# Another order of the operations of QKV, W1 and W2 on one Trainium2 core, and other staging rows in the last output block

## The chip, the cores and the metric

The kernel runs on one core of one Trainium2 chip. The time is the device time of one execution in microseconds (us). Before the change it was 1256.47 us, the median of three runs (1256.34 to 1257.6). A core has five engines with a queue of instructions each: TensorE (PE; its weight loads are shown apart as PEld), VectorE (DVE), ScalarE (ACT), GpSimd (POOL) and SyncE (SP). Each engine takes its queue strictly in order. An instruction waits for semaphores that other engines' instructions or DMA transfers raise. In this kernel SP issues nearly all transfers, and POOL issues those that add into DRAM.

## The reference

One batch of 2048 tokens with 576 channels, all in float32: a block of local attention and a block that mixes neighbouring tokens run beside each other on the same normalized input.

```python
def A(xn, wqkv, wo):      # 32 heads of 18; 8 keys back, 2 apart
    q, k, v = split(xn @ wqkv)                     # 576 -> 3 x 576
    kg, vg = k[s - 2*w], v[s - 2*w]                # w = 0..7
    attn = softmax(q . kg * 18**-0.5)              # masked where s - 2*w < 0
    return (attn . vg) @ wo                        # 576 -> 576

def B(xn, w1, w2, w3, w4):
    h = gelu(layernorm(xn) @ w1)                   # 576 -> 576
    hs = four channel quarters of h, shifted by +1, -1, +2, -2 tokens
    x1 = xn + hs @ w2
    return x1 + gelu(layernorm(x1) @ w3) @ w4      # 576 -> 4608 -> 576

xn = layernorm(x)
out = x + A(xn, wqkv, wo) + B(xn, w1, w2, w3, w4)
```

## The kernel before

**Arithmetic.** Operands of the matrix products are split into a high part (rounded to fp32r) and a low part (the rest), and a product of K rows is made from high x high, high x low and low x high. So each weight and each tile of x needs, ahead of its products: a load, a cast that gives the high part (ACT, L343 for weights, in the casts of x L579), and a subtraction that gives the low part (VectorE, L346 and L554 for weights, and for one main and one tail part at the start POOL by the same lines; VectorE, L581 and L585, for x). Rows 256 to 287 of each half of the 576 channels are the "tail" and are handled apart from the "main" rows (`wt`/`wu` for weights, `t`/`u` for x).

**Tiles.** The 2048 tokens are 16 tiles (rows of the buffer `Y`, [128, 16, 576]) of 128 tokens. For each tile of x: `x` loads it into its row of Y (SP, L298); `st` takes mean and variance (VectorE, L178 to L180) and the power -0.5 on POOL (L181); `no` normalizes in place (VectorE, L188); `ta` copies the tail channels into row 10 of Y (POOL, L362; `ta1a` on ACT); `tm` and `tt` turn main and tail through TensorE (L370, L374); `ch`, `cl`, `ct`, `cu` split the turned tile. The QKV products of tile t with a group of 432 columns are a "unit" `u`: 14 matmuls (L454), written as four parts `.0` to `.3`, then `o` (eviction from PSUM) and `s` (spill to DRAM by SP). `sc` works out the scales of the second layernorm for two tiles by seven small powers and products on POOL (L310 to L315). `sb` are four differences of weights on VectorE (L353), needed for the products of tile pairs (a Strassen-like scheme; `g6` to `g15`, TensorE L724), whose x operands are read back from DRAM (`gp`), and split again (`ph`, `pl`, `pt`, `pu`, `sx`). Then come W1 (`m`, `mg`, `mh`, `ml`), and W2 (`w0.0` and on). 39 transposes of an identity matrix (L478) run at the start ahead of the first product.

**What sets the order.** All of these operations are functions in a table `T`, and the string `ORDER_Q` (from L53) names 1108 of them in the order in which they are issued (`for name in ORDER_Q.split(): T[name]()`, L1098). That order is the order of each engine's queue. After QKV, W1 and W2 the attention and the main part of B (W3 and W4, the matmuls of L1306 and L1570, to about 1180 us) follow with an order of their own, which the change doesn't touch.

**The end.** W4's results for ten of the sixteen tiles are gathered in DRAM (`yd`): ACT evicts a partial sum from PSUM into a staging row of Y (L1311), and POOL issues a transfer that adds it to `yd` (L1312). In the last block of W3/W4 the staging rows are rows of Y that have no sum of their own at that time; `EV` holds them, and from the end of the first of its eight groups (`j == 0`) they are the rows in the tuple `rows`, taken round and round. Before that `EV` is (9, 11, 10, 2). `load_y` reads the gathered sums back into Y (SP, L1834). Then each tile of the output is the product with Wo (`mm_tok`, L272, 28 matmuls into one of three banks of PSUM), the addition of Y's row (VectorE, L1876) and the store (SP, L1877); the last tile is done in two halves (L1882).

Of the kernel before, what the change touches and what calls it, by code (L numbers as in the profile page):

```python
# [58 lines left out]
sb0.2 u4.0 u4.1 u4.2 u5.0 c1.2 wh1B11.0 tt4 tm5 ch5 u4.3 u4o u4s ct4 sb0.3 x9 cu4 u5.1 u5.2 tt5
u5.3 u5o u5s cl4 ct5 wl1B11.0 wh0T3.0 wl0T3.0 u6.0 u6.1 u6.2 u6.3 u6o u6s u7.0 aw2 wh0T1.0 u7.1  # L60
u7.2 u7.3 u7o u8.0 u9.0 u7s x6 u8.1 u8.2 x7 cu5 u9.1 wt0T3 wh0T3.1 u8.3 u8o u8s cl5 u9.2 u9.3
u10.0 wh1B11.1 st9 wl0T3.1 wu0T3 c3.0 u9o u10.1 c3.1 wt1B11 u10.2 u10.3 wl0T1.0 st6 u11.0 u10o u9s
u10s u11.1 u11.2 wh0T1.1 u11.3 u11o u11s wt0T1 c3.2 wh1B12.0 wl1B11.1 u12.0 u12.1 wu1B11 wh1B12.1
u12.2 u12.3 aw1 u12o u12s u13.0 u13.1 u13.2 u13.3 u13o x8 aw3 st7 sc6 no7 u14.0 u14.1 wl1B12.0
u13s u14.2 u15.0 u15.1 u14.3 no6 u15.2 u15.3 wl0T1.1 wu0T1 early zg6 zt6 zg7 zt7 zp3.1 u14o u14s
wl1B12.1 u16.0 wt1B12 zp3.3 wu1B12 zp3.2 sb1.0 st8 sb1.1 sb1.2 u16.1 u16.2 sb1.3 u16.3 u15o u16o
u17.0 u15s u17.1 u17.2 u17.3 no9 zp3.0 no8 aw4 u18.0 u18.1 wh1T1.0 u18.2 u18.3 wh1T3.0 wl1T3.0
u17o wl1T1.0 u16s u19.0 u19.1 u17s u18o u18s wt1T3 u19.2 sc8 zg8 u19.3 u19o u20.0 u20.1 u20.2
u20.3 u21.0 sc2 gp3.0 zt8 zg9 gp3.1 gp3.2 zt9 wh1T3.1 u21.1 gp3.3 gp3.4 u21.2 u20o u21.3 gp3.5
u21o ph3A11 wu1T3 ph3A22 zp4.2 u22.0 pl3A11 zp4.1 zp4.0 zp4.3 ph3A12 pl3A12 pl3A22 sx3.0 u19s  # L70
pt3A11 sx3.1 u23.0 pt3A22 u23.1 pt3A12 pu3A12 pu3A22 u22.1 u23.2 sx3.3 ph3S4 u23.3 u20s pl3S4
pt3S4 u22.2 pu3S4 u21s pu3A11 sx3.2 x10 u22.3 wt1T1 gp4.0 wu1T1 x11 gp4.1 gp4.2 gp4.3 gp4.4 gp4.5
ph3S1 pl3S1 pt3S1 pu3S1 wh1T1.1 wl1T1.1 aw0 u22o u23o u22s pt3S3 pu3S3 ph3S3 pl3S3 wl1T3.1 u23s
mid g6.1 g7.1 g6.5 g7.5 g6c g6.6 g6k5 g6.3 x12 g6k6 g7c g7k5 st10 st11 sc10 no10 zg10 g6.7 g6o7
g6s7 ph4A11 g6o3 g6s3 g6.2 g6o2 no11 g6s2 sx4.0 zt10 ph4A22 sx4.1 sx4.3 g7.6 g6.4 g7k6 g7.7 zg11
g6o4 pl4A11 zt11 g6s4 pt4A11 zg0 zp5.0 g7o7 zt0 zg1 pu4A11 sx4.2 g7.3 pt4A22 zp5.2 zt1 pt4S1 pu4S1
ph4S1 pl4S1 g7.2 g7o2 zg2 g7.4 g7o4 ph4A12 pl4A12 pu4A22 g7o3 pt4A12 pu4A12 g8.1 g9.1 g7s7 g8c
zp5.3 st12 zp5.1 x13 zt2 zp0.3 zp0.1 zp0.2 st13 zp0.0 sc12 gp5.0 pl4A22 gp5.1 gp5.2 sc4 gp5.3
gp5.4 gp5.5 g9c g8.5 g9.5 g9.6 g8.6 g7s2 g8.2 g8k5 pt4S3 pu4S3 ph4S3 pl4S3 x15 g8k6 g8.7 g9k5 g9k6
g8o2 g8s2 g7s4 x14 no13 no12 zg12 zt12 zg13 zt13 zp6.3 zp6.1 zp6.2 zp6.0 g8o7 zg3 g9.3 sx5.0 sx5.1  # L80
ph5S1 g8.3 g8o3 g8s3 ph5A12 g9.7 g9o7 sx5.2 ph5A11 g8.4 pl5A11 pl5S1 g9.2 g8o4 pt5A11 g7s3 g9s7
g8s7 sx5.3 pu5A11 pt5S1 g9.4 gp6.0 g9o2 st14 gp6.1 gp6.2 gp6.3 st15 g8s4 zt3 g9o4 pu5S1 g10.1
# [24 lines left out]
vh4 ml32 vl4 w0.0 rs2.3 w1.0 w1.1 mh33 mg33 ml33 w0.1 w2.0 w2.1 wy1 ws1 wy0 ws0 rs2.1 rs2.7 rg2.0
rg2.1 wy2 rg2.2 rg2.3 rp2.3 rs3.5 rs3.7 rp2.1 rs3.3 rs3.1 rg3.0 rp2.0 rg3.1 w3.0 w3.1 wy3 ws2
# [16 lines left out]
def fused_block(ctx, tc, x, wqkv, wo, w1, w2, w3, w4, out):  # L125
# [1789 lines left out]
```

## Time and profile before

| what | value |
|---|---|
| median of three runs | 1256.47 us (1256.34 to 1257.6) |
| the profiled execution, its own time | 1258.14 us |
| its span in the profile | 1256.3 us |
| TensorE busy | 99% of the span, 7361 matmuls |
| VectorE, ACT, POOL busy | 74%, 60%, 23% |
| transfers | 230.5 MB, 183 GB/s over the span |

The profile comes from one execution. A row of the timeline has the start in us, the length of the group in us, the engine, the line and operation, and the tiles that go out and in; in brackets stands how long the engine was idle before it and which engine and tile ended that. "x112" is 112 instructions in a row. A row of the stretches ("from:to") has the length, then busy time (and instructions) of PE, PEld, DVE, ACT and POOL in it, then the granted clock of TensorE (1.00 is the full clock), the share of the transfer engines, and GB/s. Lines such as L1834 are lines of the kernel before; in the changed kernel the string is a line shorter, so each line behind it has a number lower by one.

### The profile page before, as it was taken

To read this page: it belongs to the slowest core of one execution; us is meant where nothing else is said; L and a number is where in the kernel's file an instruction comes from. 1 tells how busy PE (TensorE), PEld (TensorE's weight loads), DVE (VectorE), ACT (ScalarE), POOL (GpSimd) and SP (SyncE) were. 2 spreads that over 40 slices of the span, in tenths; PEclk is the share of its full clock that TensorE was granted. 3 is DMA by queue.
4 is the path that set the end of the run, shared out by engine and by line. 5 is a ranking of instruction groups with operands and counts; after the bars stand their busy time and mean duration, and the time that the engine had idled before them with its cause. 6 is when DMAs were issued, how large, how long until landed. Compare 5 with 4: busy or idle time off the path is not lost.

```text
span 1256.3 us, 19980 instructions
## 1 busy us (share of the span) xinstructions
PE 1241.3 (99%) x7361; PEld 1144.4 (91%) x7361; DVE 931.6 (74%) x1182; ACT 759.4 (60%) x1234; POOL 285.7 (23%) x415
## 2 busy tenths in 40 slices
PE   8899999999999999999999999999999999999998
PEld 8899998899999999898899999989899999999998
DVE  7687554699458989997759898889999983554531
ACT  4456556437545545465868767776776776776610
POOL 4333100022231111111222232222232232222200
PEclk9999999999999999999999999999999999999999
DMA  7678897238788985859688998888867779899972
GB/s 211 175 183 204 191 226 213 53 113 254 183 220 195 214 168 123 168 125 255 124 180 187 211 190 191 196 167 210 235 132 178 135 140 195 175 221 229 259 226 86
DMA packets 221130, 230.50 MB, mean 183 GB/s; under 512 B 99544, under 2 KB 158136, under 8 KB 220904
## 3 DMA queue, kind: packets, MB, share of 16 engines
q1 hardware_dynamic: 188280, 162.43, 45.9%
q0 software_dynamic: 32752, 66.80, 32.7%
q8 instruction: 58, 0.95, 0.3%
q14 instruction: 40, 0.33, 0.1%
HBM read 130.76 MB, written 108.82 MB: 191 GB/s over the span
## 4 chain that ended last, share of the span: by engine, by line
PE 61%; issue 4%; DMA 4%; DVE 1%; ACT 1%; POOL 1%; SPq 0%; POOLq 0%; ACTq 0%; DVEq 0%
PE ps L1306 29%; PE cc L1570 18%; PE p L1270 10%; PE ps L272 3%; DMA yd<-Y 1%; DMA Y<-yd 1%; POOL yd L1312 1%; DMA w3st<-in_B_w_dram 1%; DMA w3s<-w3st 0%; DVE xt L970 0%; PE p L1882 0%; ACT Y L1250 0%; SPq L231 0%; DVE Y L1317 0%; DVE w3st L1403 0%
## 5 line engine op out<-in xcount | busy, mean ns | idle before, releaser
L1306 PEld LDWEIGHTS ps<-w,c 128*128 128x128 f32 x3456 | 477.8, 189 | 16.7 <-ACT Y L1311 1.6
L1306 PE MATMUL ps<-w,c 128*128 128x288 f32 x3456 | 487.3, 296 | 1.7 <-ACT Y L1311 0.9
L1312 POOL DMA_DIRECT2D yd<-Y x154 | 139.1, 906 | 366.9 <-ACT Y L1311 302.0
L1261 DVE TENSOR_TENSOR c<-Y,c 128x512 fp32r<-128x512 f32 x144 | 98.8, 687 | 87.9 <-ACT Y L1250 83.0
L1311 ACT COPY Y<-ps 128x576 f32<-128x576 f32 x154 | 97.9, 636 | 73.5 <-PE ps L1306 64.4
L1570 PE MATMUL cc<-xt,w3s 128*128 128x512 f32 (+1 forms) x504 | 127.2, 392 | 0.0
L1570 PEld LDWEIGHTS cc<-xt,w3s 128*128 128x128 f32 (+1 forms) x504 | 92.3, 188 | 17.3
L1314 ACT COPY Y<-ps 128x576 f32<-128x576 f32 x89 | 57.0, 641 | 59.0 <-PE ps L1306 57.2
L1181 DVE TENSOR_TENSOR po<-q,k 128x1152 f32<-128x1152 f32 (+1 forms) x48 | 84.2, 1755 | 0.8
L1570 PE MATMUL cc<-x1n,w3a 128*128 128x512 f32 (+1 forms) x336 | 84.7, 392 | 0.0
L1184 DVE TENSOR_REDUCE L<-po 128x64 f32<-128x1152 f32 (+1 forms) x48 | 84.0, 1751 | 0.8
L1249 ACT ACTIVATE c<-p 128x512 fp32r<-128x512 f32 x48 | 28.7, 598 | 89.1 <-PE p L1270 89.1
L1157 DVE TENSOR_TENSOR po<-v,L 128x1152 f32<-128x1152 f32 x56 | 75.4, 1354 | 0.9
L1580 DVE TENSOR_TENSOR Y<-cc,Y 128x512 f32<-128x512 f32 x49 | 33.7, 688 | 53.5 <-ACT Y L1576 47.5
L454 PE MATMUL p<-wb,xt 128*128 128x432 f32 (+1 forms) x336 | 70.9, 372 | 0.0
L1570 PEld LDWEIGHTS cc<-x1n,w3a 128*128 128x128 f32 (+1 forms) x336 | 60.4, 188 | 10.0
L454 PEld LDWEIGHTS p<-wb,xt 128*128 128x128 f32 (+1 forms) x336 | 65.5, 197 | 3.1
L1161 DVE TENSOR_TENSOR po<-po 128x1152 f32<-128x1152 f32 x49 | 66.4, 1355 | 0.9
L181 POOL TENSOR_TENSOR rs<-rs,mhalf 128x1 f32<-128x1 f32 x32 | 21.9, 686 | 170.1 <-DVE mv L184 97.0
L1287 ACT COPY ps<-Y 128x576 f32<-128x576 f32 x89 | 57.4, 645 | 3.1 <-DVE Y L1317 1.2
L724 PE MATMUL ca<-wb,xt 128*128 128x432 f32 (+1 forms) x280 | 58.9, 360 | 0.0
L724 PEld LDWEIGHTS ca<-wb,xt 128*128 128x128 f32 (+1 forms) x280 | 52.7, 189 | 2.6 <-ACT keep L731 0.2
(248 smaller groups left out, 2137.3 us busy)
## 6 DMA issues: line engine op xcount, KB each, us to landing
yd<-Y POOLq DMA_DIRECT2D x156, 288.0 KB, 6.1
Y<-in_B_w_dram SPq DMA_DIRECT2D x29, 576.0 KB, 5.7
w3st<-in_B_w_dram SPq DMA_DIRECT2D x56, 256.0 KB, 7.7
qkvd<-stg SPq DMA_DIRECT2D x44, 216.0 KB, 3.8
yd<-ev POOLq DMA_DIRECT2D x26, 288.0 KB, 6.5
w3st<-in_B_w_dram SPq DMA_DIRECT2D x92, 64.0 KB, 7.5
xd<-big SPq DMA_DIRECT2D x16, 320.0 KB, 5.6
Y<-in_A_x_dram SPq DMA_DIRECT2D x16, 288.0 KB, 3.8
```

What stands on the lines that cost most here:

```text
L454: pe.matmul(ps[:, :QB], xo[:n, o + k, a, :], W[:n, w + k, v, :], start=i == 0, stop=i == len(PLAIN) - 1)
L724: pe.matmul(ps, form(g // 2, x, n, a), W[:n, OP[w], v, :], start=start and i == 0, stop=stop and i == len(HALVES) - 1, skip_group_check=True)
L1157: dve.tensor_tensor(dst, vv, Lf[:, :, w:w + 1].to_broadcast([128, TPP * GH, HD]), op=ALU.mult)
L1161: dve.tensor_tensor(o, o, dst, op=ALU.add)
L1181: dve.tensor_tensor(dst, qf[:, None, :].to_broadcast([128, n, TPP * GC]), win, op=ALU.mult)
L1184: dve.tensor_reduce(Lw[:, w:w + n, :], dst.rearrange("p w (x d) -> p w x d", d=HD), axis=AX.X, op=ALU.add)
L1261: dve.tensor_tensor(h[:, 1, :], g, h[:, 0, :].bitcast(F32), op=ALU.subtract)
L1270: pe.matmul(ps, W3[f][:, w, :], x1n[b][:, a, :], start=n == 0, stop=n == len(PAIRS) - 1)
L1306: pe.matmul(ps[:, k, :HF], h[:, col], w[:, p, k * HF:(k + 1) * HF], start=n == 0 and not seed, stop=n == len(seq) - 1, skip_group_check=True)
L1311: act.copy(e.rearrange("p (h c) -> p h c", h=2), ps[:, :, :HF])
L1312: pool.dma_start(yd[t], e, accum_op=ALU.add)
L1570: pe.matmul(ps, WX[w][:k, v, SLOT[w], :], area[sb][xk][:k, a, :], start=onto is None and i == 0, stop=last and i == len(HALVES) - 1, skip_ ...
```

## The change

The string `ORDER_Q` is replaced as a whole. The same operations are named, in another order nearly everywhere. Its first lines are enough to see the kind:

```diff
 ORDER_Q = """
-x0 pw0 pw1 st0 x1 st1 no0 ta0 tm0 no1 tm1 x2 st2 c0.1 c0.0 zpad x3 c0.2 x4 c2.0 c2.1 c2.2 wh0B11.1
-wL0B11.1 ch0 no2 wh0B11.0 wl0B11.0 pw2 pw3 pw4 st3 tt0 cl0 ta2 tm2 ch1 cl1 x5 u0.0 ta1a u1.0 u1.1
...
+x0 st0 x1 st1 pw0 pw1 pw2 no0 x3 tm0 pw3 x2 pw4 c0.0 c0.1 c0.2 st2 ch0 x4 x5 c2.0 c2.1 c2.2
+wh0B11.0 ta0 tt0 st3 no1 tm1 wh0B11.1 no2 ct0 wl0B11.0 tm2 u0.0 ch1 u1.0 cl0 ta1a u0.2 cu0 no3 tm3
...
 """
...
         if j == 0:
             low_part(h21, Z4)
-            load_y((2, 5))
-            rows = (1, 3, 13, 15, 9)
+            load_y((1, 2, 5))
+            rows = (3, 13, 15, 9, 11)
             EV[0] = tuple(rows[(i - evc[0] - 1) % 5] for i in range(5))
...
         if j == 7:
-            load_y((1, 3))
+            load_y((3,))
```

The new order was made by a planner that takes VectorE and GpSimd to exclude each other; nothing in the kernel enforces that, and no wait is added for it. In the tail, row 1 is no longer a staging row from `j == 0` on; row 11 takes its place. Row 2 stands in `EV` ahead of `j == 0` as before. `load_y` of row 1 moves from the last group (`j == 7`) to the first.

Three places show what moves. In their rows Y_71 is the buffer Y, `wb0_125` the first weight buffer, `xt_...` the turned and split tiles of x, `ps_...` and `p1_...` are banks of PSUM, and the names in "waits" are the engines or transfer queues that are waited for.

**The start, on VectorE.** Before, rows 9 to 15 of its queue are the normalization of tiles 0 and 1, the statistics of tile 2, the normalization of tile 2, and the low part of the first weight's half:

```order
L188 TENSOR_SCALAR Y_71<-Y_71,mv0_78,rs0_81 128x576 [waits Pool_49] x2
L178 BN_STATS bn_84<-Y_71 128x6 [waits DMAHW2_49]
L178 BN_STATS bn_84<-Y_71 128x6
L179 BN_AGGR mv0_78<-bn_84 128x2 [waits DVE_49]
L180 TENSOR_SCALAR rs0_81<-mv0_78 128x1 [waits DVE_49]
L188 TENSOR_SCALAR Y_71<-Y_71,mv0_78,rs0_81 128x576 [waits Pool_49]
L346 TENSOR_TENSOR wb0_125<-rawa_221,wb0_125 128x864 [waits DMAHW4_49,Activation_49]
```

Now the statistics of tiles 3 and 2 stand between the normalization of tile 0 and that of tiles 1 and 2 (rows 9 to 19):

```order
L187 TENSOR_SCALAR Y_71<-Y_71,mv0_78,rs0_81 128x576 [waits Pool_49]
L177 BN_STATS bn_84<-Y_71 128x6 [waits DMAHW3_49]
L177 BN_STATS bn_84<-Y_71 128x6
L178 BN_AGGR mv0_78<-bn_84 128x2 [waits DVE_49]
L179 TENSOR_SCALAR rs0_81<-mv0_78 128x1 [waits DVE_49]
L177 BN_STATS bn_84<-Y_71 128x6 [waits DMAHW2_49]
L177 BN_STATS bn_84<-Y_71 128x6
L178 BN_AGGR mv0_78<-bn_84 128x2 [waits DVE_49]
L179 TENSOR_SCALAR rs0_81<-mv0_78 128x1 [waits DVE_49]
L187 TENSOR_SCALAR Y_71<-Y_71,mv0_78,rs0_81 128x576 [waits Pool_49] x2
L345 TENSOR_TENSOR wb0_125<-rawa_219,wb0_125 128x864 [waits DMAHW4_49,Activation_49]
```

So one more tile's statistics stand ahead of the normalization of tiles 1 and 2; the low part still follows the latter.

**Tiles 4 and 5, on POOL.** Before, the tail copies (L362) of tiles 4 and 5 stand apart, with the scale powers of tiles 0 and 1 (L310 to L315) between them (the first row is the power of tile 4):

```order
L181 TENSOR_TENSOR rs0_81<-rs0_81,mhalf_73 128x1 [waits DVE_49]
L362 COPY Y_71<-Y_71 128x256 [waits DVE_49,PE_49]
L181 TENSOR_TENSOR rs0_81<-rs0_81,mhalf_73 128x1 [waits DVE_49]
L310 TENSOR_TENSOR rs1_82<-rs0_81 128x2
L311 TENSOR_TENSOR rs1_82<-rs1_82,mv0_78 128x2 [waits Pool_49]
L312 TENSOR_TENSOR rs1_82<-rs1_82,eps_74 128x2 [waits Pool_49]
L314 TENSOR_TENSOR rs1_82<-rs1_82,mhalf_73 128x1 [waits Pool_49]
L315 TENSOR_TENSOR mv1_79<-rs1_82,half_75 128x1
L314 TENSOR_TENSOR rs1_82<-rs1_82,mhalf_73 128x1
L315 TENSOR_TENSOR mv1_79<-rs1_82,half_75 128x1
L362 COPY Y_71<-Y_71 128x256 [waits DVE_49,PE_49]
```

Now the power of tile 5 and both copies come first, and the power of tile 6 and the scale powers follow:

```order
L180 TENSOR_TENSOR rs0_81<-rs0_81,mhalf_73 128x1 [waits DVE_49]
L361 COPY Y_71<-Y_71 128x256 [waits PE_49,Pool_49]
L361 COPY Y_71<-Y_71 128x256 [waits DVE_49]
L180 TENSOR_TENSOR rs0_81<-rs0_81,mhalf_73 128x1 [waits DVE_49]
L309 TENSOR_TENSOR rs1_82<-rs0_81 128x2
L310 TENSOR_TENSOR rs1_82<-rs1_82,mv0_78 128x2 [waits Pool_49]
L311 TENSOR_TENSOR rs1_82<-rs1_82,eps_74 128x2 [waits Pool_49]
L313 TENSOR_TENSOR rs1_82<-rs1_82,mhalf_73 128x1 [waits Pool_49]
L314 TENSOR_TENSOR mv1_79<-rs1_82,half_75 128x1
L313 TENSOR_TENSOR rs1_82<-rs1_82,mhalf_73 128x1
L314 TENSOR_TENSOR mv1_79<-rs1_82,half_75 128x1
```

The copy of tile 5 has moved ahead of the seven small instructions. On PE, before, the tail turn of tile 4 (L374, ps_355), the main turn of tile 5 (L370, ps_437), eight products and the tail turn of tile 5 (ps_437) follow one another:

```order
L374 MATMUL ps_355<-ident_72,Y_71 128x128 [waits Activation_49,Pool_49]
L374 MATMUL ps_355<-ident_72,Y_71 128x128
L370 MATMUL ps_437<-ident_72,Y_71 128x128 [waits DVE_49,PE_49]
L370 MATMUL ps_437<-ident_72,Y_71 128x128 x3
L454 MATMUL p1_410<-wb0_125,xt_240 128x432 [waits DVE_49]
L454 MATMUL p1_410<-wb0_125,xt_240 128x432
L454 MATMUL p1_423<-wb0_125,xt_240 128x432 x6
L374 MATMUL ps_437<-ident_72,Y_71 128x128 [waits Activation_49,Pool_49]
L374 MATMUL ps_437<-ident_72,Y_71 128x128
```

Now the tail turn of tile 4 (L373, ps_339) and that of tile 5 (ps_378) have 28 products between them:

```order
L373 MATMUL ps_339<-ident_72,Y_71 128x128 [waits Pool_49]
L373 MATMUL ps_339<-ident_72,Y_71 128x128
L453 MATMUL p1_435<-wb0_125,xt_231 128x432 x8
L453 MATMUL p1_442<-wb0_125,xt_231 128x432 x6
L453 MATMUL p1_483<-wb0_125,xt_231 128x432 [waits Activation_49]
L453 MATMUL p1_483<-wb0_125,xt_231 128x432 x13
L373 MATMUL ps_378<-ident_72,Y_71 128x128 [waits Activation_49,Pool_49]
L373 MATMUL ps_378<-ident_72,Y_71 128x128
```

The tail turn of tile 5 has moved behind 20 more products; its main turn, now ps_378, stands further ahead and isn't among these rows.

**The tail, on SP.** Before, the reads of the gathered rows (L1834) stand in the order 2, 5, 7, 1, 3, with the reads of attention results (L231) between them:

```order
L231 DMA xt_11340<-xd_10773 128x3x512 [waits DMAHW2_49,PE_49]
L231 DMA xt_11340<-xd_10773 128x2x512 [waits DMAHW3_49]
L1834 DMA Y_71<-yd2_90 128x576 [waits DMASW5_49,DMAHW4_49,DMASW1_49,Activation_49]
L1834 DMA Y_71<-yd5_92 128x576 [waits DMAHW5_49,DVE_49]
L231 DMA x1n3_11530<-xd_11025 128x3x512 [waits DMAHW6_49,PE_49]
L231 DMA x1n3_11530<-xd_11025 128x2x512 [waits DMAHW7_49]
L1834 DMA Y_71<-yd7_93 128x576 [waits DMAHW0_49,DVE_49]
L231 DMA xt_11580<-xd_11244 128x3x512 [waits DMAHW1_49,PE_49]
L231 DMA xt_11580<-xd_11244 128x2x512 [waits DMAHW2_49]
L1834 DMA Y_71<-yd1_89 128x576 [waits DMAHW3_49,DMASW6_49,Activation_49]
L1834 DMA Y_71<-yd3_91 128x576 [waits DMAHW4_49,DMASW7_49,Activation_49]
```

Now row 1 is read ahead of row 2, and only row 3 stays at the end:

```order
L230 DMA xt_11340<-xd_10773 128x3x512 [waits DMAHW2_49,PE_49]
L230 DMA xt_11340<-xd_10773 128x2x512 [waits DMAHW3_49]
L1833 DMA Y_71<-yd1_89 128x576 [waits DMAHW4_49,DVE_49]
L1833 DMA Y_71<-yd2_90 128x576 [waits DMASW5_49,DMAHW5_49,DMASW1_49,Activation_49]
L1833 DMA Y_71<-yd5_92 128x576 [waits DMAHW6_49,DVE_49]
L230 DMA x1n3_11531<-xd_11025 128x3x512 [waits DMAHW7_49,PE_49]
L230 DMA x1n3_11531<-xd_11025 128x2x512 [waits DMAHW0_49]
L1833 DMA Y_71<-yd7_93 128x576 [waits DMAHW1_49,DVE_49]
L230 DMA xt_11581<-xd_11244 128x3x512 [waits DMAHW2_49,PE_49]
L230 DMA xt_11581<-xd_11244 128x2x512 [waits DMAHW3_49]
L1833 DMA Y_71<-yd3_91 128x576 [waits DMAHW4_49,DMASW6_49,Activation_49]
```

Row 1's read has moved past seven others, and it waits for VectorE and a transfer queue now, no longer for ACT's eviction into that row.

More of the change, by code (lines that the diff above doesn't have):

```diff
@@ L59 @@
[L59 to L82, printed above, removed]
```

97 lines of the change are left out of this document (60 added, 37 removed).

## The prediction

> **What bounds the kernel now.** I read the page's first part, then the busy times of four stretches that I cut at the waits, then PE's gaps in the timeline, and last the granted clock around each gap.
>
> ```profile
> PE 1241.3 (99%) x7361; PEld 1144.4 (91%) x7361; DVE 931.6 (74%) x1182; ACT 759.4 (60%) x1234; POOL 285.7 (23%) x415
> 0.00:40.00 40.00, 32.79 (x170) 30.59 (x171) 29.72 (x52) 16.03 (x28) 19.88 (x46) 0.92 0.71 187
> 40.00:344.00 304.00, 304.00 (x1671) 282.84 (x1670) 207.26 (x386) 169.83 (x301) 56.88 (x125) 1.00 0.73 182
> 344.00:1180.00 836.00, 834.61 (x5009) 761.77 (x5008) 669.24 (x716) 559.44 (x887) 204.63 (x239) 1.00 0.84 185
> 1180.00:1256.30 76.30, 69.92 (x517) 69.22 (x515) 25.36 (x31) 14.12 (x19) 4.31 (x5) 0.97 0.58 169
> ```
>
> TensorE (PE) is the bound: idle for 15.0 us of the span, 7.2 of them in the first 40 us, none in the next 304, 1.4 in the 836 after that and 6.4 in the last 76 (some 3.8 of these behind its last matmul). The change moves instructions before 344 us and in the tail; so it can only win what is lost at 0 to 40 us and in the tail, and it can lose anywhere before 344. Three gaps are large:
>
> ```profile
> 9.58 2.01 POOL L346 TENSOR_TENSOR wb<-rawa,wb 128x864 fp32r<-128x864 f32 x1
> 9.64 2.25 DVE L188 TENSOR_SCALAR Y<-Y,mv,rs 128x576 f32<-128x576 f32 x1 [0.67 <-POOL rs L181]
> 12.04 0.63 PE L370 MATMUL ps<-ident,Y 128*128 128x128 f32 x4 [2.31 <-DVE Y L188]
> 12.43 5.33 PE L454 MATMUL p<-wb,xt 128*128 128x432 f32 x18
> ...
> 33.97 1.51 DVE L353 TENSOR_TENSOR rawa<-rawa,rawb 128x1296 f32<-128x1296 f32 x1
> 34.30 1.43 POOL L362 COPY Y<-Y 128x256 f32<-128x256 f32 x1
> 35.78 0.20 PEld L374 LDWEIGHTS ps<-ident,Y 128*128 128x128 f32 x2 [3.56 <-POOL Y L362]
> 35.79 0.44 PE L374 MATMUL ps<-ident,Y 128*128 128x128 f32 x2 [3.19 <-POOL Y L362]
> ```
>
> First gap, 2.31 us: row 2's normalization, 2.25 us here, ends right after POOL's 2.01 us low part of a weight. Second gap, 3.19 us: the last tail copy on POOL (1.43 us) stands behind the scale powers on POOL, all of them beside VectorE's sums of 1.51 us. The third is in the tail, below. Each gap is paid for twice, as the clock column (PEclk) shows:
>
> ```profile
> 6.01:9.41 3.40, 3.07 (x28) 2.83 (x27) 2.42 (x8) 2.05 (x3) 1.52 (x3) 1.00 1.06 341
> 9.42:12.82 3.40, 1.09 (x9) 0.87 (x8) 3.17 (x3) 0.95 (x3) 2.16 (x2) 1.00 1.05 256
> 12.84:16.24 3.40, 3.40 (x12) 3.12 (x11) 3.23 (x9) 1.58 (x3) 1.16 (x3) 0.50 1.08 281
> 33.31:36.71 3.40, 0.92 (x6) 0.90 (x7) 3.32 (x5) 0.01 (x1) 2.42 (x2) 1.00 0.53 133
> 36.73:40.13 3.40, 3.40 (x11) 3.17 (x10) 2.64 (x4) 1.57 (x3) 0.00 (x0) 0.50 0.27 65
> 1204.09:1207.48 3.39, 1.35 (x10) 1.12 (x9) 1.41 (x2) 2.99 (x4) 0.00 (x0) 1.00 0.35 137
> 1207.50:1210.90 3.40, 3.40 (x17) 3.40 (x16) 1.79 (x3) 0.00 (x0) 0.00 (x0) 0.50 0.62 201
> ```
>
> Three windows of 3.4 us in which PE was busy for 0.92 to 1.35 us are each followed by one at clock 0.50; a window busy for 3.07 is not. What one half-clock window costs stands in the tail:
>
> ```profile
> 1190.15 4.52 SPq L1834 DMA_DIRECT2D Y<-yd  x2
> 1206.07 0.76 DVE L1876 TENSOR_TENSOR Y<-ps,Y 128x576 f32<-128x576 f32 x1 [4.72 <-DMA Y<-yd]
> 1206.88 16.41 PE L272 MATMUL ps<-Wo,xt 128*128 128x288 f32 x112 [2.04 <-DVE Y L1876]
> 1223.13 14.72 PE L272 MATMUL ps<-Wo,x1n 128*128 128x288 f32 x112
> ```
>
> 112 matmuls took 16.41 us with it and 14.72 without: **1.69 us**. The stage loses 2.04 + 1.69 here, and each gap at the start its own length and up to 1.69.
>
> ```profile
> 1169.89 1.58 SPq L231 DMA_DIRECT2D xt<-xd  x2
> 1174.75 0.86 POOL L1312 DMA_DIRECT2D yd<-Y  x1 [6.11 <-DMA x1n<-xd]
> ...
> 1223.33 0.76 DVE L1876 TENSOR_TENSOR Y<-ps,Y 128x576 f32<-128x576 f32 x1 [2.88 <-PE ps L272]
> 1226.97 0.76 DVE L1876 TENSOR_TENSOR Y<-ps,Y 128x576 f32<-128x576 f32 x1 [2.88 <-PE ps L272]
> ```
>
> **The tail: 3.73 us.** Row 1 of Y is the last staging row but one to be read back: SP asks for it at 1190.15, the add of output tile 1 gets it at 1206.07, 15.8 us later, and PE, with three banks, waits from 1204.84. In the change SP asks for row 1 first, straight behind the two reads of the second block, which it finished issuing at 1171.47 (1169.89 + 1.58), before it waits for row 2. That is over 30 us ahead of the add. What is late next: row 3, staged instead, takes row 1's place in SP's queue, so it comes at about 1206; it is due at tile 3's add, whose bank is asked for only three tiles later (adds follow each other at 3.64 us, above). Rows 2, 5 and 7 keep their places. Row 11, newly staged for the last tile, was staged before at 1174.75, 16 us earlier. The moved read of 288 KB runs while the other transfers do; at the 185 GB/s of the stretch up to 1180 it can hold others up by 1.6 us, and row 2, the first of them, has over ten us. Bounds: 0 (row 2 or 3 becomes the wait) to 3.73; I take 3.73, since every other row has slack.
>
> ```profile
> 15.97 2.05 POOL L554 TENSOR_TENSOR wb<-rawa,wb 32x864 fp32r<-32x864 f32 x1 [0.97 <-DVE Y L188]
> 18.10 0.40 POOL L362 COPY Y<-Y 128x256 f32<-128x256 f32 x1
> ```
>
> **The second gap: 4.9 us.** In the change both tail copies of rows 4 and 5 stand on POOL ahead of the scale powers, and PE asks for the second one 28 products later. Those copies follow the normalization of rows 4 and 5, not the sums, so 3.19 + 1.69 = 4.9 us go. Next late are the low parts of rows 4 and 5, now behind VectorE's four sums (6.0 us). By my count of VectorE's row durations from 10 us on they end near 33 to 35 us, and PE, at 194 ns a product, wants them near 38. The reserve is some 3 us; without it the same wait would be back. I take the new order's small waits for the tail copies at 0.4 (bounds 0 and 1.4, the 0.40 us copy behind a 1.0 us remainder of POOL's second low part): net **4.5**.
>
> **The first gap: nothing, or more.** Rows that price it:
>
> ```profile
> 6.17 0.57 DVE L188 TENSOR_SCALAR Y<-Y,mv,rs 128x576 f32<-128x576 f32 x1
> 6.33 0.82 POOL L181 TENSOR_TENSOR rs<-rs,mhalf 128x1 f32<-128x1 f32 x1 [0.52 <-DVE rs L180]
> 7.36 0.91 ACT L343 CAST wb<-rawa 128x864 fp32r<-128x864 f32 x1 [5.33 <-DMA rawa<-in_A_wqkv_dram]
> 8.66 0.92 ACT L343 CAST wb<-rawa 128x864 fp32r<-128x864 f32 x1
> 11.82 1.04 DVE L346 TENSOR_TENSOR wb<-rawa,wb 128x864 fp32r<-128x864 f32 x1
> 23.40 6.60 PEld L454 LDWEIGHTS p<-wb,xt 128*128 128x128 f32 x34
> ```
>
> The two halves of the first weight (432 KB each) were there by 7.36 and 8.66, so 432 KB take 1.3 us, and one more x tile (288 KB) ahead of them puts them at about 8.2 and 9.5. VectorE now does the statistics of rows 2 and 3 (1.2 us each, from about 6.9) before it normalizes rows 1 and 2: 9.3 to 9.9 and to 10.45, or 10.85 if POOL's power for row 3 comes between (0.82 beside a normalization). PE turns row 2 behind that and starts its products at about 11.2, not 12.43. The fifth product needs VectorE's low part (1.04). At 10.45 to 10.85 that meets POOL's low part of the other half (2.01), free to start when ACT has cast the half, at 9.5 + 0.9 = 10.4. Nothing in the code orders the two. If POOL is first, VectorE's part ends at about 13.7, PE does four products, waits 1.7 us, and goes on at 13.7; before, its fifth product was due at about 13.6, in the half-clock window. PE's waits between 8.2 and 13.7 add up to some 3 us, so a half-clock window comes again: the first gap yields **0**. If VectorE is first, PE does not wait there: about 1.5 us more, and 1.69 on top if the shorter waits (1.4 us) leave the clock whole. Bounds 0 to 3.2; below 0 by up to 1.69 if two windows are halved. I take 0, since POOL's row is ready first.
>
> The 2.25 against 0.57 us of the same normalization is the row for this. The Trainium skill, page "SBUF — State Buffer", section "Who interferes with whom", says that VectorE and GpSimd share one pair of ports, that whoever starts first keeps it for the whole instruction, and that issue order decides. By that rule the trace agrees, and a plan that only assumes the exclusion does not enforce it: 4.5 us at the start with POOL first, 6.0 to 7.7 otherwise.
>
> **From 40 to 344 us** I take nothing: PE waited for nothing in 304 us, the change has the same instructions there, and VectorE, the fullest helper, is busy for 207 us. Bounds: nothing below, 0.8 us and more above; the rival below prices it. After 344 us the waits (1.4 us) stay.
>
> **Sum.** 4.5 + 3.7 = 8.2 us. The profiled execution took 1258.14 us (its span and 1.8 around it), 0.13% over the median, so its like would take 1249.9; from the median of 1256.47 the forecast is **1248.3 us**.
>
> **Rivals.**
> 1. VectorE gets the ports first: 6.0 or 7.7 instead of 4.5, so 1246.8 or 1245.1. For it: the two start within 0.4 us by my count. Against: POOL's cast is ready at 10.4.
>
> The clock decides between these two figures. The Trainium skill, "TensorE: Matmul & The Clock Gate", Part 1, has the clock halved after an idle window of about 3.4 us. The trace halves it after windows that were 27 to 40% busy, so the page's condition is too mild a one here. By the page no window of the new start would be halved, and the sum would gain 1.7 us more (1246.6 with POOL first).
>
> 2. VectorE becomes late where the pairs' products begin, **slower than before**. Before, the first split of the first pair ran like this:
>
> ```profile
> 83.16 0.43 DVE L439 TENSOR_TENSOR xt<-xt 128x256 fp32r<-128x256 f32 x1 [1.27 <-ACT xt L432]
> 87.59 2.91 PE L724 MATMUL ca<-wb,xt 128*128 128x432 f32 x14
> ...
> 140.00:160.00 20.00, 20.00 (x104) 19.13 (x103) 9.20 (x20) 8.96 (x20) 0.00 (x0) 1.00 0.87 181
> 220.00:240.00 20.00, 20.00 (x90) 16.57 (x89) 14.31 (x20) 11.71 (x20) 0.00 (x0) 1.00 0.21 46
> ```
>
> The change puts two low parts (1.05 each) and a sum (1.51) ahead of that split, 3.6 us against 1.27 us of idle; what ACT brings forward (about 1.2 us) leaves 0 to 1.1 us of wait. Below about 2 us that costs its own length once: 1248.3 to 1249.4. If the lateness passes 2 us and returns at all five pairs, each costs 2.0 + 1.69, 18.5 in all: 1248.3 + 18.5 = 1266.8. It decides against the change from three pairs on (11 us against 8.2). Against it: later pairs have VectorE with more room, 9.2 to 14.3 us busy in 20 between 140 and 240 us.
> 3. The tail's gap stays, since row 2 or 3 takes row 1's part: 1252.0.
> 4. A new wait of 1 to 5 us elsewhere before 344 us, an input or a spill late in SP's new order: 1249.3 to 1253.3.
> 5. The start wins nothing (the copies wait for POOL again, or two windows are halved): only the tail, 1252.7.
>
> **How the numbers follow.** Forecast 0.46 (its own range 1247.0 to 1249.5), rival 1 0.22, rival 4 0.13, rival 3 0.06, rival 5 0.06, rival 2 in its slow form 0.07. The range leaves out the last and the far ends of 1 and 4: 1244.5 to 1253.5. A measurement tells this kernel from no change from about 0.2% (2.5 us) on: faster, below 1254.0, holds all but the slow form and part of 3 to 5 with small extra waits, 0.86; within 0.2% 0.07; slower 0.07.
>
> **What would show it.** Right: no PE wait on POOL's tail copy near 30 to 36 us; no window at clock 0.50 there, nor at 1207; row 1's read issued near 1165 to 1172 us; output tiles 3.64 us apart throughout the tail. POOL first shows as a VectorE low part of three us instead of one near 11 us, and a PE wait of 1 to 2 us within the first products. Wrong: any PE wait between 40 and 344 us, or a PE wait on Y in the tail.

## The result, and the profile after

| | before | after |
|---|---|---|
| median of the runs compared | 1256.40 us (8 runs, 1251.98 to 1257.6) | 1247.09 us (8 runs, 1246.07 to 1253.94) |
| ratio, 95% interval | | 0.9939 (0.9919 to 0.9959) |
| span of the profiled execution | 1256.3 us | 1246.9 us |

The change saves 9.3 us, 0.6%; forecast were 8.2. Seven of the eight runs of before lie at 1256.2 to 1257.6 us, where its runs with two windows at half clock lie (the table in the next section); in the second comparison, `after_again` below, the medians lie 7.0 us apart. First the same views as before: busy times of the page, and four stretches.

```profile
PE 1237.8 (99%) x7361; PEld 1140.0 (91%) x7361; DVE 930.1 (75%) x1182; ACT 759.4 (61%) x1234; POOL 282.8 (23%) x415
```

```profile
0.00:40.00 40.00, 37.56 (x210) 34.70 (x211) 32.41 (x61) 21.07 (x36) 20.66 (x50) 1.00 0.82 222
40.00:344.00 304.00, 303.82 (x1674) 281.44 (x1673) 203.31 (x376) 168.44 (x300) 57.24 (x128) 1.00 0.73 183
344.00:1180.00 836.00, 833.43 (x5010) 761.05 (x5009) 673.08 (x719) 558.58 (x885) 202.35 (x235) 1.00 0.84 185
1180.00:1246.90 66.90, 63.03 (x474) 62.80 (x472) 21.35 (x26) 11.32 (x15) 2.59 (x3) 1.00 0.51 168
```

In the first 40 us TensorE is idle for 2.4 us in place of 7.2, and no stretch shows a lowered clock. Where the time came from is seen by setting the start times of matmuls of the same number in the two traces against each other (worked out from the traces; 7361 matmuls in both):

| matmul number | before, us | after, us | ahead by |
|---|---|---|---|
| 100 | 22.48 | 19.08 | 3.4 |
| 200 | 46.08 | 38.13 | 8.0 |
| 1700 | 320.21 | 312.36 | 7.9 |
| 6900 | 1188.04 | 1181.44 | 6.6 |
| 7057 | 1212.73 | 1202.35 | 10.4 |
| 7337 | 1249.14 | 1239.69 | 9.5 |

So: 3.4 at the first gap, 4.6 at the second, 1.4 given back behind these, nearly all in the long stretch of W3 and W4, 3.8 in the tail, and 0.9 given back behind it. The first gap, from the timeline of the changed kernel:

```profile
8.17 0.92 ACT L342 CAST wb<-rawa 128x864 fp32r<-128x864 f32 x1
9.17 1.06 DVE L187 TENSOR_SCALAR Y<-Y,mv,rs 128x576 f32<-128x576 f32 x2
9.80 1.21 PE L369 MATMUL ps<-ident,Y 128*128 128x128 f32 x8 [0.23 <-DVE Y L187]
10.15 1.05 DVE L345 TENSOR_TENSOR wb<-rawa,wb 128x864 fp32r<-128x864 f32 x1
10.35 0.91 ACT L342 CAST wb<-rawa 128x864 fp32r<-128x864 f32 x1 [1.27 <-DMA rawa<-in_A_wqkv_dram]
10.77 3.56 PE L453 MATMUL p<-wb,xt 128*128 128x432 f32 x16
11.34 2.05 POOL L345 TENSOR_TENSOR wb<-rawa,wb 128x864 fp32r<-128x864 f32 x1 [1.07 <-DMA rawa<-in_A_wqkv_dram]
```

VectorE is first: its low part ends at 11.20, and GpSimd's begins at 11.34, since its half of the weight landed only at about 10.3. VectorE was first in all six profiles that have this start (also `after_again`, `order_only`, `late1`, `late5` and `guard`), by 0.6 to 1.6 us. Sixteen products run without a break from 10.77 on. At the second gap the copy on GpSimd and the turn that needs it now stand 15 us apart:

```profile
20.00 0.40 POOL L361 COPY Y<-Y 128x256 f32<-128x256 f32 x1 [0.38 <-DVE Y L187]
33.72 1.49 POOL L314 TENSOR_TENSOR mv<-rs,half 128x1 f32<-128x1 f32 x1
35.35 0.38 PE L373 MATMUL ps<-ident,Y 128*128 128x128 f32 x2
```

The scale powers are still slow (1.49 us, here beside VectorE's low parts; its last sum had ended at 32.0), but nothing waits for them. The tail:

```profile
1164.14 16.17 SPq L1833 DMA_DIRECT2D Y<-yd  x3
1183.18 15.07 PE L271 MATMUL ps<-Wo,x1n 128*128 128x288 f32 x112
1198.09 15.10 PE L271 MATMUL ps<-Wo,xt 128*128 128x288 f32 x112
1198.90 0.76 DVE L1875 TENSOR_TENSOR Y<-ps,Y 128x576 f32<-128x576 f32 x1 [2.75 <-DMA Y<-yd]
1213.02 15.10 PE L271 MATMUL ps<-Wo,x1n 128*128 128x288 f32 x112
```

Row 1 is asked for first of three at 1164.14. Row 3 is late now, as forecast: tile 3's addition waits for it until 1198.90. Its bank is needed by tile 6 at about 1205.6 (1183.18 + 6 x 3.73), so 5.9 us are in reserve. But tiles follow each other at 3.73 us here, where before they did at 3.64 behind the wait; that is the 0.9 us.

### The profile page after: what moved, and what is told of

The parts are those of the page before. It is cut to its first block, busy times and chain, and to the rows that moved or that the text cites. A ratio compares the mean times of both kernels' runs of the same rounds, so it can differ in the third digit from the quotient of the medians.

```text
span 1246.9 us, 19980 instructions
## 1 busy us (share of the span) xinstructions
PE 1237.8 (99%) x7361; PEld 1140.0 (91%) x7361; DVE 930.1 (75%) x1182; ACT 759.4 (61%) x1234; POOL 282.8 (23%) x415
## 4 chain that ended last, share of the span: by engine, by line
PE 66%; DMA 3%; ACT 1%; issue 1%; DVE 1%; SPq 0%; ACTq 0%; POOLq 0%
PE ps L1305 32%; PE cc L1569 20%; PE p L1269 10%; PE ps L271 4%; DMA w3st<-in_B_w_dram 1%; DMA v<-qkvd 1%; DMA xt<-td1T 1%; DMA w3s<-w3st 0%; PE p L1881 0%; ACT Y L1310 0%; ACT Y L1249 0%; DVE Y L1316 0%; DVE w3st L1402 0%; DVE xt L969 0%; SPq L1394 0%
## 5 line engine op out<-in xcount | busy, mean ns | idle before, releaser
L453 PE MATMUL p<-wb,xt 128*128 128x432 f32 (+1 forms) x336 | 68.1, 361 | 0.0
L453 PEld LDWEIGHTS p<-wb,xt 128*128 128x128 f32 (+1 forms) x336 | 62.5, 188 | 3.1 <-ACT wb L342 0.3
```

What stands on the lines that cost most here:

```text
L453: pe.matmul(ps[:, :QB], xo[:n, o + k, a, :], W[:n, w + k, v, :], start=i == 0, stop=i == len(PLAIN) - 1)
```

## The experiments

The runs of before spread widely, and that has to be understood first. 89 of them ran beside the experiments. The mean granted clock of a run falls by 0.0014 for each window of 3.41 us at half clock (3.41 / 2 / 1256). A halved window that opens behind the last matmul counts in this mean, too, though no matmul lies in it: `order_only`, `dve_low`, `small` and `after_again` have 0.999 in their profiled executions and no halved window between their first matmul and their last (in `dve_low` it begins at 1249.8 us, and the last matmul ends at 1247.7). So 0.999 can mean one window or none that costs time:

| mean granted clock of a run | before: runs, median | after (both sets): runs, median |
|---|---|---|
| 1.000 | 30, 1252.12 us | 8, 1247.09 us |
| 0.999 (one window, or only one behind the last matmul) | 12, 1254.49 us | 5, 1249.17 us |
| 0.997 (two among the matmuls) | 31, 1256.51 us | 1, 1251.21 us |
| others | 16, 1253.77 to 1264.88 us | 1, 1253.94 us |

Before runs at whole clock in a third of the cases and with two halved windows in another third, 4.4 us apart. Where both run at whole clock the change is worth 5.0 us by this table; its rows mix runs that were not made beside each other, and the one set that has both at 1.000 gives 3.4 us (`after_again`: 1249.28, 2 runs, against 1252.67, 6 runs).

**Half of the change each.** `order_only` is the change without the tail's lines (`load_y` and `rows`), `tail_only` these lines alone.

> The new order with the old tail. If the two parts are independent, it gains what the first 40 us gained, 8.0 us: 1248.4 us, with the tail's wait of 2.0 us, one half-clock window behind it and output tiles 3.64 us apart after that. The changed kernel lost about 1.4 us against before between 120 and 900 us in four small waits. If these belong to the new order, this kernel has them too and takes 1249.8 us; if they belong to the one execution, they are elsewhere or gone.

> The old order with the new tail alone. Theory 1 (the tail's wait and its half-clock window are all there is): 2.04 + 1.7 us less, 1252.7 us, output tiles 3.64 us apart. Theory 2 (the wait of before also left the matmul stream in a quicker rhythm, 130 ns a matmul in place of 133, and without the wait the slow one goes on to the end): 3.8 - 0.9 = 2.9 us less, 1253.5 us, output tiles 3.73 us apart from the first to the last, no window at half clock at the end. Both: the two gaps at the start stay as before.

`order_only`: median 1249.29 us, ratio 0.9958 (0.9940 to 0.9976). `tail_only`: 1254.42, ratio 0.9997 (0.9975 to 1.0018); among runs at whole clock 1250.49 (4 runs) against 1251.96 (13 runs beside them). So the order carries nearly all that can be measured. The tail's gain is some 1.5 us at whole clock, from four runs, less than either theory (2.9 and 3.7); over all runs it can't be told from nothing. The tail of `order_only`, from its timeline and by stretches:

```profile
1181.28 15.07 PE L271 MATMUL ps<-Wo,x1n 128*128 128x288 f32 x112
1197.88 15.19 PE L271 MATMUL ps<-Wo,xt 128*128 128x288 f32 x112 [1.53 <-DVE Y L1875]
1212.91 15.10 PE L271 MATMUL ps<-Wo,x1n 128*128 128x288 f32 x112
```

```profile
1194.11:1197.51 3.40, 2.24 (x17) 2.01 (x16) 0.44 (x1) 2.52 (x4) 0.00 (x0) 1.00 0.76 294
1197.52:1200.92 3.40, 3.04 (x23) 3.04 (x24) 2.77 (x4) 0.61 (x1) 0.00 (x0) 1.00 0.36 138
```

The wait is there (1.53 us), the half clock isn't: the wait lies across two windows, 2.24 and 3.04 us busy. And the tiles behind it stand 3.73 us apart (15.10 for four). In `tail_only` all tiles stand 3.73 us apart, by theory 2. The 1.4 us lost after 120 us were not found in `order_only` (7.9 us ahead of before at matmul 1700, 8.5 at 6900), nor in the second profile of the changed kernel, `after_again` (8.0 and 8.5): they belong to the execution, not to the order.

**The second gap alone.** `copy_only` moves one token of before:

```diff
-u3.1 ta4 u3.2 wl0B12.0 cu3 u3.3 u3o st5 no5 sc0 u2s c1.1 u3s ta5 wt0B12 ...
+u3.1 ta4 u3.2 wl0B12.0 cu3 u3.3 u3o st5 no5 u2s c1.1 u3s ta5 sc0 wt0B12 ...
```

> The kernel before with one token moved: the scale powers (sc0) stand behind the tail copy of tile 5 on GpSimd. Theory (the place of that copy on GpSimd was the second gap): the wait of 3.19 us near 36 us and the half-clock window behind it go, 4.6 us less, 1251.8 us. Rival (the new order of the products around it is needed, too): another wait takes its place within the next 10 us, for a low part of tile 4 or 5, and the gain is 0 to 2 us.

```profile
30.97 1.83 PE L454 MATMUL p<-wb,xt 96*128 96x432 f32 x8
32.64 0.38 PE L374 MATMUL ps<-ident,Y 128*128 128x128 f32 x2
```

In its trace the turn follows the products without a wait, the half clock behind it is gone, and the matmuls are 4.75 us ahead of before from number 200 to 3900: the theory's 4.6. The median is 1252.56, ratio 0.9981 (0.9959 to 1.0002); this interval just holds 1, so the trace shows the mechanism and the time alone would not.

**The first gap alone.** `dve_low` takes GpSimd's low part to VectorE in the old order:

```diff
-wL0B11.1 ch0 no2 wh0B11.0 wl0B11.0 pw2 ...
+ch0 no2 wh0B11.0 wl0B11.0 wl0B11.1 pw2 ...
```

> The kernel before with one token changed and moved: the low part of the first weight's second half is worked out on VectorE behind that of the other half, not on GpSimd, so nothing on GpSimd meets the normalization of tile 2. Theory (GpSimd's 2.0 us instruction held VectorE's normalization): the normalization takes 0.6 us, TensorE's first product begins 1.7 us sooner, and 1.7 us are won, 3.3 if the half-clock window at 12.8 goes as well: 1254.7 or 1253.1 us. Rival (VectorE is as late with the added 1.05 us): the wait moves to the first products that need a low part, and nothing is won, 1256.4.

```profile
9.36 0.58 DVE L188 TENSOR_SCALAR Y<-Y,mv,rs 128x576 f32<-128x576 f32 x1 [0.67 <-POOL rs L181]
10.90 2.03 DVE L346 TENSOR_TENSOR wb<-rawa,wb 128x864 fp32r<-128x864 f32 x2 [0.96 <-ACT wb L343]
10.92 3.32 PE L454 MATMUL p<-wb,xt 128*128 128x432 f32 x14 [0.21 <-ACT wb L343]
31.52 1.43 POOL L362 COPY Y<-Y 128x256 f32<-128x256 f32 x1
33.01 0.44 PE L374 MATMUL ps<-ident,Y 128*128 128x128 f32 x2 [1.65 <-POOL Y L362]
```

The normalization takes 0.58 us in place of 2.25, and the products begin 1.5 us sooner. No window of its start is halved, but waits of 0.5, 0.5 and 0.2 us for low parts and a cast come in its place, and TensorE is 1.2 us ahead at number 100. More than was expected came behind that: the second wait fell from 3.19 to 1.65 us, no half clock followed it, and TensorE is 4.3 us ahead at number 200. Median 1252.48, ratio 0.9989 (0.9973 to 1.0004): by the time alone not told from no change, and among runs at whole clock there is no gain (1252.26, 7 runs, against 1251.96, 13 runs beside them). In those runs of before the second wait is probably short already, since no window is halved in them; no profile here shows one, and the 1.2 us that would be left don't turn up either.

**The half clock alone.** `fill_first` brings no operand sooner; it has TensorE turn the identity matrix 12 times more in the first wait.

```diff
-... st3 tt0 cl0 ta2 tm2 ...
+... st3 tt0 pw4 pw4 pw4 pw4 cl0 ta2 tm2 ...
```

> The kernel before with 12 more transposes of the identity matrix on TensorE right ahead of the turn that waits for tile 2's normalization. They end 1.3 us later and well ahead of the wait's end, so the wait for VectorE still ends at the same time; only TensorE is busy in it. Theory (the clock is halved for one window of 3.41 us after a window of its grid in which TensorE was busy for less than about half): the window of the first gap is then some 70% busy, the next isn't halved, and 1.7 us are won although no operand comes sooner: the products from 16 us on stand 1.7 us earlier than before, the median is at 1253.5 to 1254.5. Rival (the clock falls because the wait or the start is what it is): half clock as before and nothing won; or, where TensorE's queue is what matters, 1.3 us lost.

Stretches along its clock's windows, then rows of its timeline:

```profile
9.34:12.75 3.41, 2.43 (x21) 2.20 (x20) 3.31 (x3) 1.68 (x3) 2.06 (x2) 1.00 1.03 251
12.76:16.16 3.40, 3.40 (x20) 3.21 (x19) 3.12 (x8) 1.67 (x3) 1.27 (x3) 1.00 1.06 280
29.82:33.23 3.41, 1.76 (x10) 1.36 (x9) 3.34 (x3) 1.05 (x3) 2.92 (x2) 1.00 0.67 145
33.24:36.64 3.40, 3.40 (x19) 3.25 (x19) 3.35 (x5) 1.77 (x4) 0.00 (x0) 1.00 0.41 114
```

```profile
11.86 0.63 PE L370 MATMUL ps<-ident,Y 128*128 128x128 f32 x4 [0.98 <-DVE Y L188]
26.71 0.55 POOL L314 TENSOR_TENSOR rs<-rs,mhalf 128x1 f32<-128x1 f32 x1
27.22 1.05 POOL L315 TENSOR_TENSOR mv<-rs,half 128x1 f32<-128x1 f32 x1
28.24 1.56 POOL L314 TENSOR_TENSOR rs<-rs,mhalf 128x1 f32<-128x1 f32 x1
31.31 1.43 POOL L362 COPY Y<-Y 128x256 f32<-128x256 f32 x1
32.80 0.44 PE L374 MATMUL ps<-ident,Y 128*128 128x128 f32 x2 [1.65 <-POOL Y L362]
```

The turn still starts at about 12 us (11.86), but the window ahead is 2.43 us busy in place of 1.09, and the next one keeps the whole clock. The theory holds, and it undershot: 1.5 us ahead at number 100, and 4.5 at 200, because the second wait is 1.65 us again, and its window, 1.76 us busy (52%), is not followed by a halved one. Why the second wait shrinks: the scale powers on GpSimd race with VectorE's sums. A power takes 0.55 us before the sums begin, and 1.56 beside them, one power to a sum. With TensorE on time the chain is further on when the sums begin, and the copy behind it starts at 31.31, not 34.30. Median 1251.97, ratio 0.9970 (0.9950 to 0.9991), with no operand moved. As the theory has it, the gain lies mostly in the clock: 7 of its 10 runs were at whole clock, against 6 of the 18 of before beside them, and where both were at whole clock they lie 0.8 us apart (1251.91 and 1252.67).

**Who has the ports.** `pool_first` exchanges two pairs of names in the changed kernel:

```diff
-... c0.0 c0.1 c0.2 st2 ch0 ... wh0B11.0 ta0 tt0 st3 no1 tm1 wh0B11.1 no2 ...
+... c0.1 c0.0 c0.2 st2 ch0 ... wh0B11.1 ta0 tt0 st3 no1 tm1 wh0B11.0 no2 ...
```

> The changed kernel with the two halves of the first weight exchanged in the load and in ACT's cast, so that the half whose low part GpSimd works out is there first. By the rows of the changed kernel GpSimd can begin its low part at about 10.3 us (behind a power), and VectorE's half is cast at about 11.3. Theory (the two engines exclude each other, and who begins first is done first): VectorE's low part stands at about 11.3 to 13.3 us in place of 10.2 to 11.2 (its own 1.05 behind what is left of GpSimd's 2.0), TensorE waits 1 to 2 us within its first products, a half-clock window may follow, and the time is 1 to 3.5 us over the changed kernel's: 1248 to 1250.5. Rival (they only share, or don't meet): both keep their own durations of 1.05 and about 2 us, VectorE's part ends by 12.4 and TensorE waits under 0.8 us: 1247 to 1248.

```profile
10.05 2.03 POOL L345 TENSOR_TENSOR wb<-rawa,wb 128x864 fp32r<-128x864 f32 x1
11.23 1.77 DVE L345 TENSOR_TENSOR wb<-rawa,wb 128x864 fp32r<-128x864 f32 x1 [1.06 <-ACT wb L342]
13.05 1.25 PE L453 MATMUL p<-wb,xt 128*128 128x432 f32 x5 [0.75 <-DVE wb L345]
```

GpSimd began at 10.05 and kept its 2.03 us, to 12.08. VectorE's part, ready at 11.23, took 1.77 us: 0.85 until 12.08, and its own 1.05 (the sum is 0.1 over; such rows overlap by that). TensorE waited 0.75 us there and 0.3 us for the cast; the kernel is 1.85 us behind the changed one at number 100, and the median is 1249.85, ratio 0.9971 (0.9956 to 0.9985). Exclusion, as in the theory; the Trainium skill, "SBUF — State Buffer", section "Who interferes with whom", says the same of two-input instructions of VectorE beside GpSimd's reads.

**The two small edits with the new tail.** `small` is the order of before with the edits of `dve_low` and `copy_only`, and the new tail.

> The kernel before with the two small edits at the start (low part of the second half on VectorE; scale powers behind the tail copy of tile 5) and the new tail; otherwise the old order. Theory (these three waits are all that the new order and the new tail win; the hundreds of other moves win nothing): waits of 1.7 + 3.2 + 2.0 us less than before and no half-clock window, so as fast as the changed kernel within 1 us, 1246 to 1248 us. Rival (the rest of the new order carries part of the gain, or the edits hinder each other): a wait of over 1 us on VectorE's low parts within 15 to 45 us, and 1249 us or more.

Median 1248.37, ratio 0.9950 (0.9935 to 0.9966). Its trace is 6.9 us ahead of before at number 200 where the changed kernel is 8.0. So neither theory holds quite: no wait of over 0.5 us came on the low parts, but three small edits give all but about 1 us. Whether the hundreds of other moves are worth that 1 us is not shown: the two ratios to before (0.9950 here, 0.9939 and 0.9941 for the changed kernel) have intervals that overlap. Its profiled execution was 1253.25 us for another reason, a piece of Wo that landed late for ACT in the last block:

```profile
1166.56 0.67 ACT L257 CAST Wo<-wr 128x576 fp32r<-128x576 f32 x1 [3.91 <-DMA wr<-in_A_wo_dram]
```

**A wait made in the tail.** `late1` and `late5` are the changed kernel with 11 and 17 copies like this ahead of the addition of tile 4:

```diff
+            if t == 4:
+                for _ in range(11):
+                    dve.tensor_copy(Y[:, 0, :].rearrange("p (h c) -> p h c", h=2), ps[:, :, :HF])
```

> The changed kernel with 11 more copies out of PSUM on VectorE ahead of the addition of output tile 4, so that its bank comes free late and TensorE waits about 1 us (0.4 to 2) ahead of tile 7. Theory A (a window of 3.41 us of the clock's grid is followed by one at half clock only if TensorE was busy in it for less than about half, and only the half clock changes the stream's rhythm): no half clock, tiles 3.73 us apart before and after. Theory B (any break of the stream leaves it in the quicker rhythm): 3.64 us apart after the wait.

> The same with 17 copies, so that TensorE waits about 5 us (4 to 7) ahead of tile 7. A wait that long leaves one window of the grid below half busy wherever it falls. Theory A: one or two windows at half clock follow (1.7 us each beyond the wait itself), and the tiles behind them are 3.64 us apart, as they were in the tail before. Theory C (the quicker rhythm of before's tail came from elsewhere, not from the half clock): half clock as by A, but tiles 3.73 us apart.

Timeline and stretches of `late1`, then stretches and timeline of `late5`:

```profile
1212.32 5.46 PE L271 MATMUL ps<-Wo,xt 128*128 128x288 f32 x28 [2.06 <-DVE Y L1878]
1217.62 15.10 PE L271 MATMUL ps<-Wo,x1n 128*128 128x288 f32 x112
```

```profile
1209.22:1212.62 3.40, 1.34 (x10) 1.13 (x10) 3.30 (x5) 0.00 (x0) 0.00 (x0) 1.00 0.00 0
1212.63:1216.03 3.40, 3.40 (x16) 3.40 (x15) 3.37 (x5) 0.00 (x0) 0.00 (x0) 0.50 0.33 126
```

```profile
1216.93:1220.32 3.39, 0.48 (x4) 0.25 (x2) 3.22 (x6) 0.00 (x0) 0.00 (x0) 1.00 0.00 0
1220.34:1223.74 3.40, 0.00 (x0) 0.00 (x0) 3.30 (x5) 0.00 (x0) 0.00 (x0) 0.50 0.00 0
1223.76:1227.15 3.39, 2.92 (x12) 2.96 (x13) 3.33 (x5) 0.00 (x0) 0.00 (x0) 0.50 0.23 87
```

```profile
1229.33 15.10 PE L271 MATMUL ps<-Wo,x1n 128*128 128x288 f32 x112
```

(`late1` took 1253.24 us, `late5` 1264.94, with 4.8 us of waits for late pieces of Wo and two halved windows behind them among it.) `late1`'s wait came out at 2.06 us, not 1, the same length as the tail's before; here it lay in one window (1.34 us busy), and the next was halved: the 28 matmuls took 5.46 us in place of 3.73. In `late5` (a wait of 6.8 us) both windows below half busy are followed by a halved one, of which only the second held matmuls. On the clock theory A holds in both. On the rhythm A and B fail, and C is what came: four tiles take 15.10 us behind the half clock as without it.

**Work in the new start's wait.** In `late1` the start, which is the changed kernel's, had its clock halved, too (timeline, then stretches):

```profile
9.60 0.44 PE L373 MATMUL ps<-ident,Y 128*128 128x128 f32 x2 [1.70 <-POOL Y L361]
```

```profile
7.72:11.12 3.40, 1.47 (x11) 0.93 (x10) 3.26 (x11) 1.05 (x2) 1.83 (x3) 1.00 1.08 267
11.13:14.53 3.40, 3.40 (x13) 2.87 (x11) 2.57 (x4) 3.26 (x6) 2.23 (x2) 0.50 1.04 343
```

`guard` fills that wait (`-... ta0 tt0 st3 ...`, `+... ta0 pw4 pw4 pw4 tt0 st3 ...`).

> The changed kernel with 9 more transposes of the identity matrix on TensorE ahead of tile 0's tail turn, where it waits 0.8 us in the changed kernel's profile and waited 1.7 us in late1's, whose window was 43% busy and was followed by one at half clock. They take about 1.0 us. Theory (the new start, too, is halved in some executions, and work in its wait keeps it from that): a wait as short as 0.8 us is filled with nothing lost beyond 0.2 us, a longer one leaves its window over half busy; runs at whole clock as before near 1247 to 1249, fewer runs below it than the 7 of 15 of the changed kernel, ratio to before 0.991 to 0.995. Rival (the runs below whole clock come from late pieces of Wo and the like in the last block): the same spread of clocks as the changed kernel, ratio as it had (0.994).

Median 1248.39 us (12 runs), ratio 0.9955 (0.9931 to 0.9980); 5 of 12 runs below whole clock, against 7 of 15; at 0.998 or less, where a window among the matmuls is certain, 3 of 12 against 2 of 15. So the rival holds, or too few of these runs come from the start to show it; nothing is won over the changed kernel.

**Both once more.**

> The changed kernel once more, on the chip and beside the runs of this set. If its gain is waits (5 us) plus the half-clock windows that the old waits bring in most runs (up to 3.4 to 5 us more), its own runs are mostly at whole clock, near 1247, and those of before spread over 1251 to 1258 by their clock. If the first comparison was a matter of the chip, the ratio moves out of 0.992 to 0.996.

> The kernel before once more, for a second profile. If the quicker rhythm behind the tail's wait (tiles 3.64 us apart in place of 3.73) belongs to the wait for row 1 or to the half clock behind it, it comes again where the clock is halved there; if it was chance, tiles stand 3.73 us apart to the end.

`after_again`: 1249.21 us (7 runs) against 1256.21 (18 runs), ratio 0.9941 (0.9919 to 0.9963), so the ratio of the first comparison stands. The expected level does not: two of the seven runs were at 1.000 and five at 0.999, around 1249 and not 1247 us; why is open. `before_again` took 1258.71 us; its tail, by stretches:

```profile
1204.28:1207.68 3.40, 2.31 (x18) 2.08 (x16) 0.43 (x1) 2.54 (x4) 0.00 (x0) 1.00 0.75 288
1207.69:1211.09 3.40, 3.03 (x22) 3.03 (x23) 2.78 (x4) 0.59 (x1) 0.00 (x0) 1.00 0.36 137
```

A wait of 1.47 us, no half clock, tiles 3.73 us apart: neither the halved window nor the quicker rhythm of the first profile came again in the tail.

## Why the prediction was right, point by point

- **The second gap (4.5 us): right.** 4.6 in the trace, 4.75 with the one token of `copy_only`. None of the small waits (0.4) came. But the gaps were added up as if each stood alone, which they don't: 1.5 of the second gap's 3.19 us hung on the first (`fill_first`, `dve_low`), and the two edits that win 4.3 and 4.75 us alone win 6.9 together (`small`).
- **The first gap (0, GpSimd first): wrong; rival 1 came in its dearer form, 3.4 us for its 3.2.** The step that failed is "POOL's row is ready first". VectorE's low part began at 10.15, not at 10.45 to 10.85, and the cast of GpSimd's half ended at 11.26, not 10.4, because the half landed 0.8 us later than the 1.3 us per half gave. Those 1.3 us lay between two casts of ACT before; the second one (8.66) shows no wait for a transfer and stands behind another cast of ACT, so it doesn't tell when its half landed. The mechanism itself was right, as `pool_first` shows: with GpSimd first, 1.85 us of it are lost.
- **"Each gap is paid for twice": right as a mechanism, mis-sized in the tail.** In the one profile it read, it was so three times. The first gap was followed by half clock in all four profiles that kept it as it was (before, `tail_only`, `copy_only`, `before_again`), but 30 of the 89 runs of before show no halved window at all, so this price, too, is paid in some executions only. In the tail it was halved in one of six profiles with the old tail (before, `before_again`, `order_only`, `copy_only`, `dve_low`, `fill_first`), whose waits of 1.5 to 2.0 us mostly straddled two windows. So the term of 3.73 is typically 1.5 to 2.0, which agrees with the 1.5 of `tail_only` at whole clock.
- **The tail's mechanism: right.** The wait is gone, row 3 is late in row 1's place with 5.9 us to spare, no other row waits. "Output tiles 3.64 us apart throughout" was wrong: 3.73.
- **Nothing from 40 to 344 us: right** (0.2 us idle); rivals 2 to 5 did not come. The 1.4 us lost later were of this execution.

The forecast lay 1.2 us over the measured time since the first gap (3.4 more than forecast) outweighed what the tail and the long stretch gave back (0.9 and 1.4). That these errors nearly cancel is luck, and so is part of the agreement in size: the terms were read off one execution of before with all three windows halved, and the runs of before in the first comparison lie mostly where two are.

## What to carry to other kernels

A wait costs its length, and half a clock window more if it leaves one window of the clock's grid below about half busy. The grid isn't tied to the kernel (the transposes at the start speed up from one in 0.21 us to one in 0.11 us at a time between 4.2 and 7.3 us, by the profile, and the later halved windows lie on the grid that begins there), so one profile shows one throw: read the granted clock of many runs before a stage is priced. Where a wait can't be removed, cheap work on TensorE inside it can remove the second price and whatever hangs on the delay, as in `fill_first`; in `guard`, where the wait was shorter, it won nothing.

Two engines that exclude each other are best kept apart by what is ready when; a change of 1 us in a landing decides who goes first, and so about 2 us (1.85 in `pool_first`).

## What the runs showed of the hardware that was not expected

- **The clock's rule.** Halved windows of one execution stand whole multiples of 3.413 us apart (12.83, 36.72, 1207.49 before). All fourteen profiles were laid on their grids. Between the first matmul and the last, windows at whole clock that were up to 43% busy (0 to 1.48 us) were followed by one at half clock, and windows from 49% on (1.68 us and up) were not. The Trainium skill, "TensorE: Matmul & The Clock Gate", Part 1, has the free-running window of 3413 ns, with which the traces agree, and an idle window as the condition, which is too mild: a window 40% busy is enough.
- **A halved window feeds the next wait.** A wait near 33 us was 3.2 us where a window at 13 us had been halved (before, `tail_only`, `before_again`) and 1.65 where none had been (`fill_first`, `dve_low`), by the rows through the race of GpSimd's powers with VectorE's sums.
- **A quicker rhythm, open.** Behind the tail's wait the first profile of before ran its 288-column matmuls at 130 ns each; everywhere else each fourth one takes 9 ns more (133 on average). Neither a wait (`order_only`, `before_again`) nor a wait with a halved window (`late1`, `late5`) brought it back; what did is not known. It made the tail of that one execution 0.9 us shorter.
